# Start addresses of the matrix products' operands in SBUF: probabilities 192 bytes past a multiple of 256, token tiles 16 bytes past one

## The chip, the core and the metric

The kernel runs on one core of one Trainium2 chip. The metric is device time in microseconds of one execution; lower is better. Engines go by their short names: PE is TensorE's matrix products, PEld its loads of the stationary operand, DVE VectorE, ACT ScalarE, POOL GpSimd, SP SyncE, which issues the transfers.

## What is computed

Eight sequences of 576 tokens and eight heads of 64 columns go through an attention over 32 memories a head, and its output through a feed-forward block, all in float32:

```
a    = softmax(phi)                      # 576 x 32 a head
k_m, v_m = a^T k, a^T v                  # 32 x 64 a head
attn = softmax(q k_m^T / 8)              # 576 x 32 a head: "the probabilities"
x    = attn v_m                          # heads side by side: 4608 x 512
h    = x @ w_in                          # 512 -> 2048
out  = (h * clip(h + 3, 0, 6) / 6) @ w_out   # 2048 -> 512
```

## The kernel before, in words

For each of the 8 sequences (b) the kernel first folds the memories into the first weight matrix: `fold` (L367) multiplies v_m with a chunk of w_in, and the result, split into a high and a low part, is the tile `both` (L385, L393). So the first product can take the probabilities themselves as its moving operand.

The work is a list of 140 slots. A slot is one block of 128 of the 2048 hidden columns (index f). In 124 slots, all in one precision, these steps run:

- `gemm1` (L427) is the first product. It has 12 matrix products on PE, each with a load of a 128 by 128 stationary part of `both`: six have the probabilities of the first 256 tokens as moving operand (tiles `phi0`, `plo0`: high part, low part, 256 columns), six those of the last 320 tokens (`phi1`, `plo1`, 320 columns). For each half the order is high by high twice, low by high twice, high by low twice.
- `relu` (L449, ACT), `gate` (L453, DVE) and `gate_rest` (L459, ACT) turn the result into the gated tile `gf`, 128 by 576. The last 64 tokens of each sequence go to `rest` and are worked on later in 16 slots of their own, which have no first product.
- `high` (L468, ACT) and `low` (L473, DVE) split 512 tokens of `gf` into `ghi` and `glo`, each four token tiles of 128.
- `gemm2` (L480) is the second product, two slots later (`LAG = 2`): 12 products of 512 columns, each with a token tile of `ghi` or `glo` as the stationary operand and a part of w_out (`w2`, in the profile named `w`) as the moving one. First the four tiles of `ghi` with the high part of w_out, then the same four with its low part, then the four of `glo` with the high part.

The last four of the 16 slots of `rest` use `gemm2_by_columns` (L507) instead, with 256 columns a product: 96 products, the last work of the kernel.

The order of all steps is written out by hand: a string `BEGIN` for the start and a table `STEADY` for what is played between the steps of each slot. The first eight slots are "plain": they use unsplit float32, where each product passes twice (tiles `pT` and `gp`). A few products (`warm`, L627, bf16) fill PE at the start.

Tiles of a pool stand one behind the other in each partition of SBUF, so that a tile's start address follows from the sizes of the tiles ahead of it. In the kernel before, `threes` (16 words, of which one is used) and `maxima` (a slice of a wider tile) stand ahead of others.

Of the kernel before, what the change touches and what calls it, by code (L numbers as in the profile page):

```python
# [10 lines left out]
F32 = mybir.dt.float32  # L11
F32R = mybir.dt.float32r
# [7 lines left out]
B, H, S, D, M = 8, 8, 576, 64, 32  # L20
DM, DF = 512, 2048
P = 128
# [4 lines left out]
NG = 2  # L27
# [6 lines left out]
KV = 2 * D + 1  # L34
EPS = 1e-9
LAG = 2
VC = 256
VW_RING = {"tag": "vw", "bufs": 6}
TMP = {"tag": "tmp", "bufs": 3}
# [57 lines left out]
def attention_ffn_kernel(ctx: ExitStack, tc: tile.TileContext, pn, pt, kv, kl, qt, w1, w2, out):  # L97
    nc = tc.nc
    cpool = ctx.enter_context(tc.tile_pool(name="cpool", bufs=1))
    wpool = ctx.enter_context(tc.tile_pool(name="wpool", bufs=1))  # L100
    xpool = ctx.enter_context(tc.tile_pool(name="xpool", bufs=1))
# [29 lines left out]
    def magnitude(*u):  # L131
        sizes[u] = sb.tile([P, UNIT], U32, name="tmp", **(O_RING if u in ((1, 0), (1, 1)) else TMP))
        for cols, high, _ in raw[u]:
            nc.scalar.activation(sizes[u][:, cols].bitcast(F32), high.bitcast(F32), AF.Abs)  # L134
# [12 lines left out]
    def sign(*u):  # L147
        for cols, high, _ in raw[u]:
            size_ = sizes[u][:, cols]
            nc.vector.scalar_tensor_tensor(size_, high, 0xC0000000, size_, ALU.bitwise_and, ALU.bitwise_or)  # L150
# [55 lines left out]
    class Attention:  # L206
# [178 lines left out]
        def folded_high(self, c, k):  # L385
            both = vw[self.b, FC // VC * c + k] = wpool.tile([P, 2, NG, VC], F32R, name="both", **VW_RING)
            nc.scalar.copy(both[:, 0], self.pv[c][:, :, VC * k : VC * (k + 1)])  # L387

        def folded(self, c, k):
            both = vw[self.b, FC // VC * c + k] = wpool.tile([P, 2, NG, VC], F32R, name="both", **VW_RING)  # L390
            nc.scalar.copy(both[:, 0].bitcast(F32), self.pv[c][:, :, VC * k : VC * (k + 1)])

        def folded_low(self, c, k):  # L393
            both = vw[self.b, FC // VC * c + k]
            src = self.pv[c][:, :, VC * k : VC * (k + 1)]
            nc.vector.tensor_tensor(both[:, 1], src, both[:, 0].bitcast(F32), ALU.subtract)  # L396
# [11 lines left out]
    class Slot:  # L408
# [44 lines left out]
        def gate(self):  # L453
            relu = self.gf
            if self.plain:
                self.gf = wpool.tile([P, 4 * P], F32, name="gp", tag="ghi", bufs=LAG + 1)[:, : self.n]
            nc.vector.scalar_tensor_tensor(self.gf, relu, 6.0, self.h, ALU.min, ALU.mult)  # L457

        def gate_rest(self):  # L459
# [6 lines left out]
            return self.gf[:, : len(self.tiles) * P]  # L466

        def high(self):  # L468
            self.ghi = wpool.tile([P, 4 * P], F32R, name="ghi", tag="ghi", bufs=LAG + 1)
            nc.scalar.copy(self.ghi[:, : len(self.tiles) * P], self.gated())  # L470

        def low(self):
            self.glo = wpool.tile([P, 4 * P], F32R, name="glo", tag="glo", bufs=LAG + 1)  # L473
            n = len(self.tiles) * P
            nc.vector.tensor_tensor(self.glo[:, :n], self.gated(), self.ghi[:, :n].bitcast(F32), ALU.subtract)  # L475

# [176 lines left out]
    def play(words):  # L653
        for word in words:
            name, *args = word.split(".")
            n = [int(x) for x in args]
            if name in WEIGHTS:
                WEIGHTS[name](*n)
            elif name in SLOT:
                SLOT[name](slots[n[0]], *n[1:])  # L660
            elif name in LOADS:
                LOADS[name](*n)
            else:
                ATTENTION[name](atts[n[0]], *n[1:])
# [25 lines left out]
    def laid_out(first, last, rows):  # L690
        said = []
        for n in range(first, last):
            s = slots[n]
            said += [f"{x}.{n}" for x in ("h" if s.rest else "gumkh" if 1 in s.hfs else "gumh")]
            for w in rows.get(n, ()):
                said += group(w)
            said.append(f"l.{n}")
            if n >= LAG:
                said += [f"a.{n - LAG}"] + slots[n - LAG].ends(n - LAG)
        return said  # L700

    def table(text, start):
        rows = {}
        for line in text.split("/"):
            words_ = line.split()
            if words_:
                rows.setdefault(start + int(words_[0]), []).extend(words_[1:])
        return rows

    with tc.manual_schedule():  # L710
        ident = cpool.tile([P, P], F32, name="ident")
        make_identity(nc, ident)
        ones = cpool.tile([P, P], F32, name="ones")
        nc.vector.memset(ones, 1.0)

        threes = xpool.tile([P, M // 2], F32, name="three")
        nc.vector.memset(threes, 3.0)
        three = threes[:, :1]

        maxima = cpool.tile([P, 3 * M], F32, name="maxima")[:, : NG * M]  # L720
        nc.vector.memset(maxima, 0.0)

        rest = wpool.tile([P, NFT, P], F32, name="rest")
        nc.vector.memset(rest[:, :NJ], 0.0)  # L724

        play(BEGIN.split())
        n = starts[5]
        for b in range(2, B + 1):
            if b > 2 and b % 2 == 0:
                play(laid_out(n, n + NFT // 4, {}))  # L730
                n += NFT // 4
            if b < B:
                rows = table(STEADY.replace("C", str(b)).replace("N", str(b + 1)).replace("M", str(b + 2)), n)
                for k in rows:
                    rows[k] = [w for w in rows[k] if int(w.split(".")[1]) < B]
                play(laid_out(n, n + NFT, rows))
                n += NFT
        for k in range(n - LAG, n):
            play([f"a.{k}"] + slots[k].ends(k))
# [49 lines left out]
```

## Time and profile before

| what | us |
|---|---|
| three runs | 714.71, 714.26, 714.60; median 714.6 |
| the profiled execution | 714.73, of which span 712.9 |
| PE busy | 703.4 of 712.9 |
| PEld busy | 561.8 |
| DVE, ACT, POOL busy | 383.0, 325.7, 105.6 |
| granted TensorE clock | 1.0 over the whole span |

The profiled execution lasts 1.8 us longer than its span and 0.1 us longer than the median of the runs. A matrix product is a pipeline: its recorded length is longer than the distance to the next one's start, and its end is modelled. So a product's price is read from the distances between starts, or from a piece of the chain of waits divided by its count, and not from the mean length of one.

### The profile page before, as it was taken

To read this page: it belongs to the slowest core of one execution; us is meant where nothing else is said; L and a number is where in the kernel's file an instruction comes from. 1 tells how busy PE (TensorE), PEld (TensorE's weight loads), DVE (VectorE), ACT (ScalarE), POOL (GpSimd) and SP (SyncE) were. 2 spreads that over 40 slices of the span, in tenths; PEclk is the share of its full clock that TensorE was granted. 3 is DMA by queue.
4 is the path that set the end of the run, shared out by engine and by line. 5 is a ranking of instruction groups with operands and counts; after the bars stand their busy time and mean duration, and the time that the engine had idled before them with its cause. 6 is when DMAs were issued, how large, how long until landed. Compare 5 with 4: busy or idle time off the path is not lost.

```text
span 712.9 us, 11655 instructions
## 1 busy us (share of the span) xinstructions
PE 703.4 (99%) x4806; PEld 561.8 (79%) x4806; DVE 383.0 (54%) x593; ACT 325.7 (46%) x626; POOL 105.6 (15%) x73
## 2 busy tenths in 40 slices
PE   9999999999999999999999999999999999999997
PEld 4456777888878787878788887888888888788887
DVE  4899986765453554545534455535544354343331
ACT  4677785643343443434434344534344344443331
POOL 1645331430100310013000120002100031000000
PEclk9999999999999999999999999999999999999999
DMA  9997682645230804153320532128041211130002
GB/s 348 420 344 284 197 284 87 245 145 188 114 141 16 348 2 163 60 208 140 129 94 16 197 152 105 59 92 316 1 163 60 74 60 60 60 118 1 1 1 74
DMA packets 25149, 99.21 MB, mean 139 GB/s; under 512 B 2696, under 2 KB 3720, under 8 KB 20488
## 3 DMA queue, kind: packets, MB, share of 16 engines
q1 hardware_dynamic: 25016, 98.40, 37.0%
q8 instruction: 38, 0.62, 0.4%
q14 instruction: 15, 0.12, 0.1%
q10 hardware_dynamic: 80, 0.07, 0.0%
HBM read 82.72 MB, written 15.73 MB: 138 GB/s over the span
## 4 chain that ended last, share of the span: by engine, by line
PE 93%; DVE 4%; ACT 1%; issue 1%; POOL 1%; ACTq 0%; POOLq 0%
PE acc L497 53%; PE ph L441 28%; PE pv L376 4%; PE acc L627 3%; PE pk L271 2%; PE acc L516 2%; PE psc L309 1%; DVE gf L457 1%; DVE tmp L142 1%; ACT gf L451 0%; DVE glo L475 0%; POOL w L171 0%; PE pq L293 0%; DVE w L171 0%; DVE tmp L150 0%
## 5 line engine op out<-in xcount | busy, mean ns | idle before, releaser
L497 PE MATMUL acc<-w,ghi 128*128 128x512 f32 x1088 | 282.0, 397 | 0.0
L497 PEld LDWEIGHTS acc<-w,ghi 128*128 128x128 f32 x1088 | 197.5, 188 | 65.4 <-ACT gf L451 15.1
L457 DVE SCALAR_TENSOR_TENSOR gf<-gf,ph 128x576 f32<-128x576 f32 x124 | 93.3, 753 | 185.7 <-ACT gf L451 185.2
L451 ACT ACTIVATE gf<-ph,three 128x576 f32<-128x576 f32 (+2 forms) x132 | 95.8, 727 | 197.9 <-PE ph L441 193.0
L441 PE MATMUL ph<-phi,both 128*128 128x256 f32 x992 | 174.1, 297 | 2.1 <-DVE gf L457 2.0
L441 PEld LDWEIGHTS ph<-phi,both 128*128 128x128 f32 x992 | 150.9, 188 | 16.2 <-DVE gf L457 4.5
L497 PE MATMUL acc<-w,glo 128*128 128x512 f32 x544 | 150.3, 389 | 0.0
L497 PEld LDWEIGHTS acc<-w,glo 128*128 128x128 f32 x544 | 102.1, 188 | 21.3
L475 DVE TENSOR_TENSOR glo<-gf,ghi 128x512 fp32r<-128x512 f32 x124 | 88.5, 715 | 39.7 <-ACT ghi L470 36.6
L441 PE MATMUL ph<-plo,both 128*128 128x256 f32 x496 | 105.7, 294 | 0.0
L441 PEld LDWEIGHTS ph<-plo,both 128*128 128x128 f32 x496 | 78.5, 188 | 0.0
L470 ACT CAST ghi<-gf 128x512 fp32r<-128x512 f32 x124 | 76.0, 616 | 4.6 <-PE acc L497 3.6
L461 ACT COPY rest<-gf 128x64 f32<-128x64 f32 x124 | 30.2, 245 | 86.5 <-DVE gf L457 86.5
L396 DVE TENSOR_TENSOR both<-pv,both 128x512 fp32r<-128x512 f32 x62 | 42.7, 689 | 49.8 <-ACT both L387 49.6
L339 POOL TENSOR_TENSOR st<-st,mx 128x512 f32<-128x512 f32 (+1 forms) x16 | 22.8, 1423 | 287.6 <-DVE mx L335 287.6
L387 ACT CAST both<-pv 128x512 fp32r<-128x512 f32 x62 | 36.1, 584 | 23.6 <-DVE both L396 18.2
L376 PE MATMUL pv<-w,kvT 64*32 64x512 f32 (+1 forms) x528 | 35.1, 588 | 1.0 <-DVE pnat L254 0.6
L364 POOL TENSOR_TENSOR plo<-pT,phi 128x512 fp32r<-128x512 f32 (+1 forms) x14 | 21.3, 1526 | 56.2 <-ACT phi L359 56.2
L351 POOL TENSOR_TENSOR st<-st,sm 128x512 f32<-128x512 f32 (+1 forms) x15 | 19.6, 1304 | 63.6 <-DVE sm L347 52.2
L160 POOL TENSOR_TENSOR w<-tmp,raw 128x512 uint32<-128x512 uint32 x14 | 21.8, 1576 | 45.3 <-DVE tmp L150 24.9
L627 PE MATMUL acc<-rest,ident 128*128 128x512 bf16 x82 | 22.1, 421 | 1.7 <-DVE rest L724 1.7
L134 ACT ACTIVATE tmp<-raw 128x512 f32<-128x512 f32 (+1 forms) x24 | 18.9, 831 | 6.2 <-DMA raw<-in_w 6.2
(77 smaller groups left out, 425.7 us busy)
## 6 DMA issues: line engine op xcount, KB each, us to landing
w<-w_kept SPq DMA_DIRECT2D x24, 1024.0 KB, 6.7
kvt<-in_kv SPq DMA_DIRECT2D x32, 516.0 KB, 8.6
raw<-in_w SPq DMA_DIRECT2D x16, 512.0 KB, 8.9
raw<-in_w SPq DMA_DIRECT2D x8, 1024.0 KB, 10.2
out_t<-o SPq DMA_DIRECT2D x16, 512.0 KB, 3.0
qh<-in_qt SPq DMA_DIRECT2D x8, 640.0 KB, 10.1
ptile<-in_pt SPq DMA_DIRECT2D x8, 576.0 KB, 3.8
pnat<-in_pn SPq DMA_DIRECT2D x8, 576.0 KB, 4.7
```

Of the source, the lines that this page charges most:

```text
L339: (engine or nc.gpsimd).tensor_tensor(st, st, self.over_memories(hf, "mx"), ALU.subtract)
L376: nc.tensor.matmul(to[j * M : (j + 1) * M, g, k], self.kvT[rows, g, j * M : (j + 1) * M], chunk[rows, k, j].bitcast(F32), start=True, stop ...
L387: nc.scalar.copy(both[:, 0], self.pv[c][:, :, VC * k : VC * (k + 1)])
L396: nc.vector.tensor_tensor(both[:, 1], src, both[:, 0].bitcast(F32), ALU.subtract)
L441: nc.tensor.matmul(dst, w[:, g, fs], x[:, g * n : (g + 1) * n], start=(i == 0), stop=(i == len(seq) - 1),)
L451: nc.scalar.activation(self.gf, self.h, AF.Relu, bias=three)
L457: nc.vector.scalar_tensor_tensor(self.gf, relu, 6.0, self.h, ALU.min, ALU.mult)
L461: nc.scalar.copy(kept, self.gf[:, self.n - REST :])
L470: nc.scalar.copy(self.ghi[:, : len(self.tiles) * P], self.gated())
L475: nc.vector.tensor_tensor(self.glo[:, :n], self.gated(), self.ghi[:, :n].bitcast(F32), ALU.subtract)
L497: nc.tensor.matmul(accs[self.b, self.rest, k], left[:, t * P : (t + 1) * P], w, start=k in self.first and k not in begun, stop=k in self.l ...
L627: nc.tensor.matmul(fill["out"], ident.bitcast(BF16)[:, :P], fill["in"], start=True, stop=True)
```

## The change

No instruction is added, removed or moved on any engine; one fill at the start, of `three`, is 1 column wide where it was 16. The start addresses of tiles change, through the widths of the tiles ahead of them, and `ghi` and `glo` begin 4 words inside their tiles.

```diff
+AHEAD = 4
...
             if self.plain:
-                self.gf = wpool.tile([P, 4 * P], F32, name="gp", tag="ghi", bufs=LAG + 1)[:, : self.n]
+                self.gf = wpool.tile([P, 4 * P + 64], F32, name="gp", tag="ghi", bufs=LAG + 1)[:, : self.n]
...
         def high(self):
-            self.ghi = wpool.tile([P, 4 * P], F32R, name="ghi", tag="ghi", bufs=LAG + 1)
+            self.ghi = wpool.tile([P, 4 * P + 64], F32R, name="ghi", tag="ghi", bufs=LAG + 1)[:, AHEAD : AHEAD + 4 * P]
...
         def low(self):
-            self.glo = wpool.tile([P, 4 * P], F32R, name="glo", tag="glo", bufs=LAG + 1)
+            self.glo = wpool.tile([P, 4 * P + 64], F32R, name="glo", tag="glo", bufs=LAG + 1)[:, AHEAD : AHEAD + 4 * P]
...
-        ones = cpool.tile([P, P], F32, name="ones")
+        ones = cpool.tile([P, P + M], F32, name="ones")[:, :P]
...
-        threes = xpool.tile([P, M // 2], F32, name="three")
-        nc.vector.memset(threes, 3.0)
-        three = threes[:, :1]
-
-        maxima = cpool.tile([P, 3 * M], F32, name="maxima")[:, : NG * M]
+        three = xpool.tile([P, 1], F32, name="three")
+        nc.vector.memset(three, 3.0)
+
+        maxima = xpool.tile([P, NG * M + 40], F32, name="maxima")[:, : NG * M]
```

In the two built programs the operands of the products stand at these bytes past a multiple of 256, in each of their buffers and at each start of a part of them (the parts of a tile lie multiples of 256 bytes apart):

| operand | moving or stationary | before | now |
|---|---|---|---|
| `phi0`, `plo0` (first product, 256 columns) | moving | 64 | 192 |
| `phi1`, `plo1` (first product, 320 columns) | moving | 0 | 0 |
| `both` (first product) | stationary | 0 | 0 |
| w_out's parts (second product) | moving | 0 | 0 |
| `ghi`, `glo` (second product) | stationary | 0 | 16 |
| w_in's chunks (fold) | moving | 0 | 0 |
| `kvT` (fold, scores) | stationary | 0, 128 | 128, 0 |
| `qh` (scores) | moving | 224 | 96 |

The tiles of the attention, which stand behind all others, move up by 1664 bytes together, so `gf`, `st` and `pT`, the key and value tiles and the output tiles are 128 bytes further round.

## Rows read from the trace of the kernel before

**Rows 1.** The page's busy time, share of the span and instructions of each engine, then the granted clock in 40 slices.

```profile
PE   703.4 (99%) x4806; PEld 561.8 (79%) x4806; DVE 383.0 (54%) x593; ACT 325.7 (46%) x626; POOL 105.6 (15%) x73
...
PEclk9999999999999999999999999999999999999999
```

**Rows 2.** The page's chain that ended last, as shares of the span by line (its first entries).

```profile
PE acc L497 53%; PE ph L441 28%; PE pv L376 4%; PE acc L627 3%; PE pk L271 2%; PE acc L516 2%; PE psc L309 1%; DVE gf L457 1%; DVE tmp L142 1%; ACT gf L451 0%; DVE glo L475 0%; POOL w L171 0%; PE pq L293 0%; DVE w L171 0%; DVE tmp L150 0%
```

**Rows 3.** Groups of instructions by line and shape: operation, count, busy us, mean ns of one, idle time before.

```profile
L497 PE MATMUL acc<-w,ghi 128*128 128x512 f32 x1088 | 282.0, 397 | 0.0
L497 PE MATMUL acc<-w,glo 128*128 128x512 f32 x544 | 150.3, 389 | 0.0
L441 PE MATMUL ph<-phi,both 128*128 128x256 f32 x496 | 80.3, 284 | 2.1 <-DVE gf L457 2.0
L441 PE MATMUL ph<-plo,both 128*128 128x256 f32 x248 | 49.2, 279 | 0.0
L441 PE MATMUL ph<-phi,both 128*128 128x320 f32 x496 | 93.8, 310 | 0.0
L441 PE MATMUL ph<-plo,both 128*128 128x320 f32 x248 | 56.5, 309 | 0.0
L457 DVE SCALAR_TENSOR_TENSOR gf<-gf,ph 128x576 f32<-128x576 f32 x124 | 93.3, 753 | 185.7 <-ACT gf L451 185.2
L475 DVE TENSOR_TENSOR glo<-gf,ghi 128x512 fp32r<-128x512 f32 x124 | 88.5, 715 | 39.7 <-ACT ghi L470 36.6 <-PE acc L497 2.4
L470 ACT CAST ghi<-gf 128x512 fp32r<-128x512 f32 x124 | 76.0, 616 | 4.6 <-PE acc L497 3.6 <-DVE gf L457 0.7
L376 PE MATMUL pv<-w,kvT 64*32 64x512 f32 x496 | 33.8, 601 | 0.6 <-DVE pnat L254 0.6
L627 PE MATMUL acc<-rest,ident 128*128 128x512 bf16 x82 | 22.1, 421 | 1.7 <-DVE rest L724 1.7
```

**Rows 4.** Busy time of each engine in stretches of the span (us from its start: length, then busy us and count of PE, PEld, DVE, ACT, POOL, granted clock, DMA share, GB/s).

```profile
50.00:75.00 25.00, 24.14 (x226) 17.05 (x226) 24.22 (x37) 17.98 (x34) 9.74 (x6) 1.00 0.72 260
75.00:100.00 25.00, 23.25 (x143) 18.04 (x142) 22.69 (x33) 19.13 (x36) 9.53 (x6) 1.00 0.71 253
100.00:125.00 25.00, 24.72 (x216) 19.96 (x215) 17.66 (x26) 16.17 (x27) 5.33 (x3) 1.00 0.45 147
125.00:150.00 25.00, 25.00 (x172) 20.09 (x171) 18.92 (x23) 14.08 (x30) 12.71 (x6) 1.00 0.75 265
...
200.00:300.00 100.00, 100.00 (x755) 82.34 (x754) 50.09 (x81) 41.91 (x85) 8.50 (x6) 1.00 0.34 128
```

**Rows 5.** The timeline of PE over two whole slots in a row with nothing between them: start us, length us, line, operation, count merged into the row. The distance from one row's start to the next row's start, divided by the count, is the price of one product.

```profile
244.96 0.64 PE L441 MATMUL ph<-phi,both 128*128 128x256 f32 x4
245.43 0.40 PE L441 MATMUL ph<-plo,both 128*128 128x256 f32 x2
245.67 0.76 PE L441 MATMUL ph<-phi,both 128*128 128x320 f32 x4
246.26 0.46 PE L441 MATMUL ph<-plo,both 128*128 128x320 f32 x2
246.55 2.00 PE L497 MATMUL acc<-w,ghi 128*128 128x512 f32 x8
248.40 1.07 PE L497 MATMUL acc<-w,glo 128*128 128x512 f32 x4
249.30 0.64 PE L441 MATMUL ph<-phi,both 128*128 128x256 f32 x4
249.78 0.40 PE L441 MATMUL ph<-plo,both 128*128 128x256 f32 x2
250.01 0.76 PE L441 MATMUL ph<-phi,both 128*128 128x320 f32 x4
250.61 0.46 PE L441 MATMUL ph<-plo,both 128*128 128x320 f32 x2
250.90 2.00 PE L497 MATMUL acc<-w,ghi 128*128 128x512 f32 x8
252.74 1.07 PE L497 MATMUL acc<-w,glo 128*128 128x512 f32 x4
253.65 0.64 PE L441 MATMUL ph<-phi,both 128*128 128x256 f32 x4
```

**Rows 6.** Pieces of the chain of waits, in order of time: start us, length us, line, products in the piece. These are stretches of the second product alone: the slots of `rest`, and at the end the 96 products of 256 columns.

```profile
185.94 10.91 PE acc L497 x48
...
358.34 13.63 PE acc L497 x60
...
697.80 11.52 PE acc L516 x96
```

**Rows 7.** The timeline of PE at 23 us, columns as in rows 5: 24 warm products in bf16, 512 columns, that wait for nothing.

```profile
23.15 5.35 PE L627 MATMUL acc<-rest,ident 128*128 128x512 bf16 x24
```

## Prediction

> **What bounds the kernel now.** First the busy times: PE is busy 703.4 of 712.9 us at a granted clock of 1.0 throughout, which is the level of 2.4 GHz [rows 1]. Then the chain that ended last: 53% of it is the second product (L497) and 28% the first (L441), and no other line has over 4% [rows 2]. Then the stretches: from 125 us on PE is busy for the whole of each, while DVE and ACT are busy about half the time; only up to 125 us is PE short of work, by 0.3 to 1.8 us in each 25 [rows 4]. So nothing but the pace of PE's products counts from 125 us on, and the change can work by that pace alone: it adds and removes no instruction.
>
> The pace stands in the timeline of two slots [rows 5]. A slot takes 4.34 us (244.96 to 249.30, and 4.35 to 253.65). From starts to starts: the six products of 256 columns 0.71 us, 118.3 ns each; the six of 320 columns 0.88 us, 146.7 each; the twelve of 512 columns 2.75 us, 229 each. Of these twelve the eight with `ghi` take 1.85 us, 231 each, and the four with `glo` 0.90 us, 225 to 227 each.
>
> Is that already the least possible? The warm products in bf16 show what 512 columns cost when the stream isn't disturbed: 24 of them last 5.35 us, and one alone is recorded at 421 ns [rows 3, 7], so (5.35 - 0.42) / 23 = 214 ns. In proportion, 320 columns would take 134 and 256 columns 107. What the float32 products take above that is the quantity that this change is about, and it shows a pattern:
>
> - moving and stationary operand both at a multiple of 256: 512 columns in a long stretch of the second product take 10.91 / 48 = 227.3 and 13.63 / 60 = 227.2 ns; 320 columns 146.7; 256 columns in the tail (L516) 11.52 / 96 = 120.0 [rows 5, 6]. That is 13 ns above the undisturbed pace, in all three, whatever the number of columns. A cost per product that does not grow with its columns belongs to what happens once per product, and that is the load of its 128 stationary columns, which reads SBUF while the product before it streams.
> - moving operand at 64, stationary at 0: 256 columns take 118.3, so 11 ns above.
> - the eight products after the change from the first to the second product take 231, 4 more than in a long stretch.
>
> I read this as the stream being held up by the load that runs beside it, with a price that depends on how their addresses stand to each other. That is an inference: addresses are in no row, and only two pairings of them (0 with 0, 64 with 0) occur in this precision.
>
> **The change part by part.** Two pairings are new: the second product's goes from (0, 0) to (0, 16), the first half's of the first product from (64, 0) to (192, 0).
>
> The second product, 1088 + 544 = 1632 products [rows 3]. Upper bound of the gain: the whole excess goes, 229 - 214 = 15 ns by 1632 = 24.5 us. The other end: nothing excludes that 16 is a worse pairing than 0; the nearest dearer price is the one behind a change of product, 231 on all of them, (231 - 229) by 1632 = 3.3 us lost, and if the excess doubled, 13 ns by 1632 = 21 us lost, for which no row speaks. What I take: in the only comparison of two pairings at one width, leaving 0 was worth 120.0 - 118.3 = 1.7 ns, and I give that to every product, 2.8 us. I also let the dearer start of each slot go, because a stream that doesn't run into the load has nothing to settle into: 8 products by 4 ns by 124 slots = 4.0 us. Together 6.8 us less.
>
> The first half of the first product, 496 + 248 = 744 products [rows 3]. 192 is 64 short of a multiple where 64 is 64 past one. Between the ends of (118.3 - 107) by 744 = 8.4 us gained and, back to the price of pairing (0, 0), 1.7 by 744 = 1.3 us lost, I take 0, since the distance from the multiple is the same.
>
> The second half of the first product, 744 products, keeps its pairing: 0. The 96 products of the tail go with the second product: at 1.7 ns 0.2 us gained, at most 13 by 96 = 1.2 us.
>
> The fold (L376) keeps its moving operand, and its stationary tile goes round by 128 bytes. Its 496 products of 512 columns are unsplit float32 and run several at a time (33.8 us busy for 496 with a mean of 601 ns [rows 3]); 4% of the chain is theirs [rows 2]. I take 0; a twentieth of that share, 1.4 us either way, is the bound. Writes and reads of the moved tiles by DVE and ACT are covered: `gf`, `ghi` and `glo` cost them 753, 616 and 715 ns of a slot of 4340 [rows 3, 5], so even some tens of ns more each would stay under PE. The narrower fill of `three` is one instruction at the start: 0. If PE gets faster by 55 ns a slot (6.8 us over 124), ACT and DVE go from about half busy to half busy and one percent, and nothing is late next. Before 125 us a part of the gain is lost, since PE waits there for DVE anyway: the 75 us from 50 to 125 hold at most 75 / 4.34 = 17 of the 124 slots, 0.9 us of the gain, and I count half of that as lost.
>
> Sum: -6.8 - 0.2 + 0.5 = -6.5 us against the profiled execution's 714.7, so 708.2. The median of the runs stands 0.1 below that execution: **708** us.
>
> **The rivals.**
>
> *The load is cleared out of the stream's way altogether.* If one line of 16 bytes between the two is the step that matters, most of the excess goes: between half and all of 24.5 us in the second product, with up to 8.4 in the first half, -13 to -33 us, 682 to 702. For it: the excess is the same 13 ns at 512, 320 and 256 columns, so it looks like one cause that can be avoided. Against it: 64 bytes, a far larger step, took away 2 of the 13.
>
> *Addresses do nothing.* The 1.7 ns between tail and first half may come from the lines themselves: the tail's products write other banks and follow another order. Then the time stays within a microsecond of 714.6.
> The Trainium skill (SBUF, "Who interferes with whom") says that PE has two read ports, one for the moving operand and one for the load of the stationary one, independent of each other, and that PE never waits on anyone; by that rule this rival is the one to expect. The trace doesn't agree as it stands: a load costs the stream 13 ns here, though it does not say through which part of the memory.
>
> *Slower: 16 bytes is a start from which the stream meets the load more often.* The place is the second product, from its first slot in this precision to the end. If both advance through the same memory, the load starting one step ahead may put it just where the stream arrives; then the dear first products of a slot last for all twelve (231 or more), and the first half falls back to 120. At 231 that is 3.3 + 1.3 us, 719; at half as much excess again, 6.5 by 1632 = 10.6 us and 1.3 more, 726.5. It decides from about 1 ns more per product (1.6 us). For it: the dear start shows that this price can rise without any change of address. Against it: the one step away from 0 that the trace has made things cheaper.
>
> **How the numbers follow.** A measurement of this kernel tells changes from about 0.2%, 1.4 us. Forecast, a gain of 1.5 to 13 us (702 to 713): 0.44. All or most of the excess gone (682 to 702): 0.22. No effect, 713 to 716: 0.13. Slower, 716 to 727: 0.21. So faster 0.66, the same 0.13, slower 0.21. For a range that leaves out 2 in 10, I cut the lower half of the case of the full gain and the upper third of the slower one: 690 to 721.
>
> **What would show it.** In the profile after, the twelve products of a slot should take 2.65 to 2.70 us from start to start instead of 2.75, the pieces of 48 and 60 products 225 to 226 ns each instead of 227.3, and the eight with `ghi` should no longer be dearer than the four with `glo`; the six products of 256 columns should stay at 0.71 us, those of 320 columns at 0.88. If the long pieces fall to 215 to 220 each, the first rival is right; if a slot keeps 4.34 us, the second; if the piece of 48 is above 11.0 us, the third. The prediction is wrong as a whole if the time moves while these distances don't, for instance by a transfer or a wait before 125 us.

## The result and the profile after

| | median | range | runs |
|---|---|---|---|
| before | 714.65 us | 714.26 to 715.18 | 6 |
| after | 718.74 us | 718.20 to 719.42 | 6 |

The change makes the kernel slower: ratio 1.0058, interval 1.0045 to 1.0071, 4.1 us. The forecast was 708 us and faster. The time is that of the slower rival, 719.

Lines of the kernel after stand one further down: L442 is the first product, L498 the second, L517 the 96 products at the end. The page of the kernel after, busy times, granted clock, and the chain by engine and by line:

```profile
PE 706.8 (99%) x4802; PEld 561.0 (78%) x4806; DVE 382.7 (53%) x593; ACT 325.9 (45%) x626; POOL 105.7 (15%) x73
...
PEclk9999999999999999999999999999999999999999
...
PE 91%; DVE 4%; DMA 2%; ACT 1%; issue 1%; SPq 1%; POOL 1%; ACTq 0%; POOLq 0%
PE acc L498 53%; PE ph L442 27%; PE pv L377 4%; PE pk L272 2%; PE acc L517 2%; DMA kvt<-in_kv 1%; PE psc L310 1%; PE acc L628 1%; DVE tmp L143 1%; DMA raw<-in_w 1%; DVE gf L458 0%; DVE glo L476 0%; POOL w L172 0%; PE pq L294 0%; ACT gf L452 0%
```

The bound is the same as in [rows 1, 2]: PE, at the same clock, with 3.4 us more of busy time. DVE and ACT have not moved. The row of the stretches that answers to [rows 4] (length, then busy us and count of PE, PEld, DVE, ACT, POOL, granted clock, DMA share, GB/s) has PE without a gap again:

```profile
125.00:150.00 25.00, 25.00 (x172) 19.88 (x171) 18.38 (x23) 13.87 (x28) 12.74 (x6) 1.00 0.76 271
```

Two groups of the page (line, operation, shape and count; busy us, mean ns) answer to [rows 3]:

```profile
L498 PE MATMUL acc<-w,ghi 128*128 128x512 f32 x1088 | 285.7, 400 | 0.0
L498 PE MATMUL acc<-w,glo 128*128 128x512 f32 x544 | 153.0, 394 | 0.0
```

So it is the second product that has grown, by 3.7 and 2.7 us. How it pays shows in one slot of PE's timeline (start us, length us, what, count), as in [rows 5]:

```profile
249.98 0.64 PE L442 MATMUL ph<-phi,both 128*128 128x256 f32 x4
250.45 0.40 PE L442 MATMUL ph<-plo,both 128*128 128x256 f32 x2
250.68 0.74 PE L442 MATMUL ph<-phi,both 128*128 128x320 f32 x4
251.27 0.46 PE L442 MATMUL ph<-plo,both 128*128 128x320 f32 x2
251.56 2.03 PE L498 MATMUL acc<-w,ghi 128*128 128x512 f32 x8
253.43 1.09 PE L498 MATMUL acc<-w,glo 128*128 128x512 f32 x4
254.35 0.63 PE L442 MATMUL ph<-phi,both 128*128 128x256 f32 x4
```

From start to start the slot takes 4.37 us, 0.03 more. The first product's two halves take 0.70 and 0.88 (before 0.71 and 0.88; as medians over the kernel 707 and 876 ns, before 710 and 888), the second product 2.79 (before 2.75). The eight with `ghi` take 1.87, 234 ns each, the four with `glo` 0.92, 230 each: what were dear products at the start of a slot are now twelve dear products. The long stretches in the chain of waits (start us, length us, what, count) say it most plainly:

```profile
186.11 11.19 PE acc L498 x48
...
359.70 13.99 PE acc L498 x60
529.28 13.99 PE acc L498 x60
...
701.73 11.38 PE acc L517 x96
```

11.19 / 48 = 233.1 and 13.99 / 60 = 233.2 ns, where [rows 6] has 227.3 and 227.2. The starts of these pieces show where the loss comes in: 0.17 us by the first (185.94 before), 1.36 by the second (358.34), 3.93 by the last (697.80). From 186 us on it is spread evenly over all that PE paces. Of these stretches only that of the 96 products of 256 columns got cheaper, 118.5 ns each for 120.0.

In the tables below, times of the second product are distances between starts in the trace, as medians, sorted by what PE did just ahead of it: "plain" where that was the first product (62 times; four more, with another step right behind them, are left out), "behind another step" where it was a fold, scores or another step of the attention (49 times).

| kernel | `phi0`; tiles at | plain | behind another step |
|---|---|---|---|
| before | 64; 0 | 2749 ns | 2851 ns |
| after | 192; 16 | 2791 | 2906 |

Summed from 186 us on, each against its counterpart in the kernel before, that is 2.1 us for 50 plain ones, 2.1 for 43 others and 1.2 for the long stretches; the first product gives 1.6 back and the last 96 products 0.1. Together 3.7, and the chain shows 3.6 (3.93 - 0.17 - 0.14).

### The profile page after: what moved, and what is told of

The parts are those of the page before. It is cut to its first block, busy times and chain, and to the rows that moved or that the text cites. A ratio compares the mean times of both kernels' runs of the same rounds, so it can differ in the third digit from the quotient of the medians.

```text
span 716.7 us, 11651 instructions
## 1 busy us (share of the span) xinstructions
PE 706.8 (99%) x4802; PEld 561.0 (78%) x4806; DVE 382.7 (53%) x593; ACT 325.9 (45%) x626; POOL 105.7 (15%) x73
## 4 chain that ended last, share of the span: by engine, by line
PE 91%; DVE 4%; DMA 2%; ACT 1%; issue 1%; SPq 1%; POOL 1%; ACTq 0%; POOLq 0%
PE acc L498 53%; PE ph L442 27%; PE pv L377 4%; PE pk L272 2%; PE acc L517 2%; DMA kvt<-in_kv 1%; PE psc L310 1%; PE acc L628 1%; DVE tmp L143 1%; DMA raw<-in_w 1%; DVE gf L458 0%; DVE glo L476 0%; POOL w L172 0%; PE pq L294 0%; ACT gf L452 0%
## 5 line engine op out<-in xcount | busy, mean ns | idle before, releaser
L498 PE MATMUL acc<-w,ghi 128*128 128x512 f32 x1088 | 285.7, 400 | 0.0
L498 PEld LDWEIGHTS acc<-w,ghi 128*128 128x128 f32 x1088 | 198.4, 189 | 67.2 <-ACT gf L452 15.1
L442 PE MATMUL ph<-phi,both 128*128 128x256 f32 x992 | 172.4, 296 | 1.9 <-DVE gf L458 1.8
L442 PEld LDWEIGHTS ph<-phi,both 128*128 128x128 f32 x992 | 149.0, 188 | 16.7 <-DVE gf L458 4.4
L498 PE MATMUL acc<-w,glo 128*128 128x512 f32 x544 | 153.0, 394 | 0.0
L498 PEld LDWEIGHTS acc<-w,glo 128*128 128x128 f32 x544 | 102.8, 189 | 23.7
L442 PE MATMUL ph<-plo,both 128*128 128x256 f32 x496 | 105.9, 295 | 0.0
L442 PEld LDWEIGHTS ph<-plo,both 128*128 128x128 f32 x496 | 79.3, 188 | 0.0
L377 PE MATMUL pv<-w,kvT 64*32 64x512 f32 (+1 forms) x528 | 35.1, 588 | 0.9 <-DVE pnat L255 0.6
```

The lines of the kernel that those rows point to most:

```text
L377: nc.tensor.matmul(to[j * M : (j + 1) * M, g, k], self.kvT[rows, g, j * M : (j + 1) * M], chunk[rows, k, j].bitcast(F32), start=True, stop ...
L442: nc.tensor.matmul(dst, w[:, g, fs], x[:, g * n : (g + 1) * n], start=(i == 0), stop=(i == len(seq) - 1),)
L498: nc.tensor.matmul(accs[self.b, self.rest, k], left[:, t * P : (t + 1) * P], w, start=k in self.first and k not in begun, stop=k in self.l ...
```

## The experiments

**1. One part alone, and other starts for the token tiles.** Four kernels, all edits of one number in the changed kernel.

Only the probabilities move (tiles back at 0):

```diff
-AHEAD = 4
+AHEAD = 0
```

> The changed kernel with the token tiles back at a multiple of 256; the probabilities of the first 256 tokens stay 192 past one. Theory (two separate prices: the second product's 512-column products cost 6 ns more with the stationary at 16, the first product 15 ns less a slot with its moving operand at 192): a product in the long stretches falls back to 227 ns, 48 of them to 10.9 us, the first product keeps 1.58 us, and the time is about 2 us below the kernel before, 712.5 to 713.2. Rival (the loss comes with the shift of all the other tiles, by 128 bytes for the attention's and by 256 modulo 512 for the weights'): the long stretches stay at 233 ns and the time stays near 718.7.

Measured: 712.87 us, ratio 0.9975 (0.9966 to 0.9984). Faster by 1.8 us, as expected. The second product takes 2745 ns plain and 2853 behind another step, close to before; the first product 1582 for 1598. The long pieces of 60 are back at 13.62 us with all the other tiles still shifted, so the rival, the shift of the other tiles, is out.

Only the tiles move (probabilities back at 64):

```diff
-        maxima = xpool.tile([P, NG * M + 40], F32, name="maxima")[:, : NG * M]
+        maxima = xpool.tile([P, NG * M + 8], F32, name="maxima")[:, : NG * M]
```

> The changed kernel with the probabilities of the first 256 tokens back at 64 past a multiple of 256 (and so the attention's tiles back where they stood modulo 256); the token tiles stay 16 past. Theory (two separate prices): the second product stays at 233 ns in the long stretches, the first product goes back to 1.60 us a slot, and the time is some 2 us above the changed kernel, 720 to 721. Rival (the shift of the other tiles is the loss): near the kernel before, 714.6.

Measured: 716.32 us, ratio 1.0021 (1.0012 to 1.0030). Slower than before, but by 1.6 us only, where 720 to 721 was expected: a miss. -1.8 and +1.6 alone make +4.1 together, so prices don't add, and one price per pairing of addresses can't be the whole of it. The chain of waits of this run (start us, length us, what, count) shows why:

```profile
242.89 3.00 PE acc L498 x12
245.89 1.56 PE ph L442 x12
247.44 2.72 PE acc L498 x12
250.16 1.60 PE ph L442 x12
251.76 2.79 PE acc L498 x12
254.55 1.56 PE ph L442 x12
256.11 2.72 PE acc L498 x12
```

The same twelve products from the same kind of addresses take 2.72 us in one slot and 2.79 in the next; 33 of the 62 plain ones are at 2.72. Neither time is that of the kernel before, 2.75.

The tiles at 64 and at 32 instead of 16 (`AHEAD = 16`, `AHEAD = 8`):

> The changed kernel with the token tiles 64 bytes past a multiple of 256 in place of 16. Theory A (any start away from the moving operand's breaks a steady state that holds at equal starts, so each is dearer): 230 ns or more a product in the long stretches, 716 to 722. Theory B (the price depends on the distance, with cheap and dear ones; 64 was 2 ns cheaper than 0 for 256 columns): 222 to 226 ns, 706 to 712.

> The changed kernel with the token tiles 32 bytes past a multiple of 256 in place of 16. Theory A (any start away from the moving operand's is dearer): 230 ns or more a product in the long stretches, 716 to 722. Theory B (the price depends on the distance): something other than both 227 and 233 ns; if it rises steadily from 16 to 32, above 236 ns and above 722; if it falls towards 64, below 230 and below 717.

Measured: 718.58 us, 1.0054 (1.0040 to 1.0068), and 718.09 us, 1.0047 (1.0034 to 1.0061). Plain second products take 2803 and 2798 ns. Both times are those of theory A, and 16 isn't special as a step; but that any start away from 0 is dearer is already contradicted by half the slots of the run above.

**2. The pairings by themselves.** A kernel of products alone, with no other engine at work: 20 products from one pair of start addresses, then the next pair, for 512, 256 and 320 columns. It and the two kernels like it below ran once each.

```diff
+        for m in (0, 4):
+            for k in range(16):
+                for n in range(REPEAT):
+                    t = n % 4
+                    nc.tensor.matmul(acc[:, t], sta[k][:, t * P : (t + 1) * P], mov[m], start=n < 4, stop=n >= REPEAT - 4)
+                leave()
```

> The disputed price by itself: a kernel that leaves out the reference's work and only runs sequences of 20 float32 products, each sequence with a short wait ahead of it, the stationary operand at 0, 16, ... 240 bytes past a multiple of 256, the moving one at 0 or 64 (512 columns), at 0, 64, 128 or 192 (256 columns), at 0 (320 columns). Theory B (the settled price of a product depends on the pairing of addresses alone): at 512 columns 227 ns for (0, 0), 233 for stationary 16 and 32, 233 for 64, and the same table for any moving start when the stationary is counted from it; then one stationary start is the cheapest for all widths, and it is worth 6 to 12 ns a product below 227 if there is a cheap one. Theory C (a pairing has several steady states, and the way into the sequence chooses): prices jump between a few values (113, 117 or 120 at 256 columns; 227 or 233 at 512) without order in the stationary's start, and differ from those in the kernel at the same pairing.

PE's timeline of this run (the names tell how many bytes past a multiple of 256 the moving and the stationary operand start):

```profile
21.10 4.80 PE L50 MATMUL acc<-mov_zero,sta_sixteen 128*128 128x512 f32 x20 [0.25 <-ACT sink L44]
26.22 4.93 PE L50 MATMUL acc<-mov_zero,sta_thirtytwo 128*128 128x512 f32 x20 [0.31 <-ACT sink L44]
...
182.96 2.65 PE L56 MATMUL acc<-mov_zero,sta_zero 128*128 128x256 f32 x20 [0.31 <-ACT sink L44]
...
194.72 2.55 PE L56 MATMUL acc<-mov_zero,sta_sixtyfour 128*128 128x256 f32 x20 [0.31 <-ACT sink L44]
```

With everything else silent the addresses alone change the pace: (4.93 - 4.80) / 19 = 7 ns a product at 512 columns. The settled distances are 226.7 (moving at 0 with stationary at 16 or 240, both at 64) to 234 ns at 512 columns, 113.4 (stationary 64 bytes past moving, at three of the four moving starts) to 120.0 (equal starts, and some others) at 256, 144.5 to 146.7 at 320. Two things follow. None of the 32 pairings at 512 columns goes below 226.7. And 0 with 16, the pairing of the change, is among the cheapest here, although it is dear in the kernel. So the pairing alone doesn't set the price.

**3. Whole slots by themselves.** The twelve products of a slot's first product and the twelve of its second, six slots for each setting (`both`, `phi0`, tiles, in words of 4 bytes), no other engine at work.

```diff
+        for b, p, t in ((0, 16, 0), (0, 16, 0), (0, 48, 0), (0, 16, 4), (0, 48, 4), (16, 0, 0), (0, 0, 0)):
+            for k in range(SLOTS):
+                first_product(b, p)
+                second_product(t, k == 0, k == SLOTS - 1)
```

> PE alone: six slots in a row of first product (six of 256 columns, six of 320) and second product (twelve of 512), with nothing else running and no wait inside, for seven settings: probabilities at 64 with tiles at 0 (twice, the first while the clock may still rise), 192 with 0, 64 with 16, 192 with 16, then the folded weights at 64 with probabilities and tiles at 0, and last all at 0. It leaves out the reference's work. Theory (the pace is settled by PE's own stream and its loads, and a pairing can have two steady states between which the products ahead of it choose): once settled a slot takes 4.35 us for 64 and 0, 4.33 for 192 and 0, 4.37 for 192 and 16, and for 64 and 16 either about 4.29 or 4.38, as in the whole kernels; with the folded weights at 64 about 4.31; with all at 0 4.35. Rival (other engines' reads and writes of SBUF hold the stream up): without them every setting takes about the same, near 4.1 us.

Measured: the settled slots take 4347 ns with 64 and 0 (before), 4327 with 192 and 0, 4373 with 192 and 16 (after), the same as in the whole kernels, whose slots take 4347, 4327 and 4373. Other engines and transfers have no part in it, and that rival is out. The six products of 320 columns, none of whose own addresses differ, take 887 ns behind probabilities at 64 and 875 behind probabilities at 192. With the folded weights at 64 the slot takes 4333 ns, where 4310 was expected. With 64 and 16 there is no single settled slot (PE's timeline of this run):

```profile
95.27 0.87 PE L47 MATMUL h<-phi_sixtyfour,both_zero 128*128 128x256 f32 x6
95.97 1.05 PE L49 MATMUL h<-last_zero,both_zero 128*128 128x320 f32 x6
96.86 2.95 PE L53 MATMUL acc<-w_zero,tiles_sixteen 128*128 128x512 f32 x12
99.65 0.84 PE L47 MATMUL h<-phi_sixtyfour,both_zero 128*128 128x256 f32 x6
100.33 1.04 PE L49 MATMUL h<-last_zero,both_zero 128*128 128x320 f32 x6
101.21 2.88 PE L53 MATMUL acc<-w_zero,tiles_sixteen 128*128 128x512 f32 x12
103.93 0.87 PE L47 MATMUL h<-phi_sixtyfour,both_zero 128*128 128x256 f32 x6
```

2.79 us (96.86 to 99.65), then 2.72 (101.21 to 103.93), and so on in turn. The addresses are the same in both; what differs is how the products ahead went (the six of 256 columns 0.70 and 0.68 us, those of 320 columns 0.89 and 0.88). So the sequence carries something over from product to product, which I call its state.

**4. Other addresses for the first product.** The folded tile `both` at 64, with the probabilities and tiles at 0; and everything at 0.

```diff
+    def folded_tile():
+        n = 2 * NG * VC
+        both = wpool.tile([P, n + 64], F32R, name="both", **VW_RING)
+        return both[:, BOTH_AT : BOTH_AT + n].rearrange("p (k g v) -> p k g v", k=2, g=NG)
```

> Folded weights (the first product's stationary operand) 64 bytes past a multiple of 256, all other operands of the two products at a multiple: the pairing that settled at 113.4 ns for 256 columns by itself, beside 117.8 for the one of the kernel before. Theory (prices measured alone hold in the kernel): 256 columns settle at 113 to 115 ns, a slot is 20 to 30 ns shorter than in the kernel before, and the time is 711 to 712.5, the fastest so far. Rival (how the sequence is entered decides): the six products of 256 columns stay at 117 to 120 and the time is within 1.5 us of 714.6.

> All operands of the two products at a multiple of 256, the probabilities of the first 256 tokens too. Theory (prices by pairing): 256 columns at 120 ns in place of 118.3, no dearer start of the 320 columns behind them, since the pairing doesn't change there; 1.3 us lost on the first and 0.9 to 1.2 gained on the second: 714 to 716. Rival (leaving the multiple was worth more, because a change of pairing resets the sequence): above 717.

Measured: 713.55 us, 0.9983 (0.9974 to 0.9992), a miss by 1 us; and 714.52 us, 0.9998 (0.9989 to 1.0007), as expected, though by smaller terms: the products of 256 columns are 3 ns a slot dearer (713 for 710), those of 320 columns 6 cheaper (882 for 888), the second product 4 cheaper. The miss has the same cause as that of experiment 1: I carried the 113.4 ns of 20 products in a row over to six products behind the second one, and there they take 117 to 118.

**5. All settings of a slot.** The same whole slots, five each, for 209 settings of `phi0`, `phi1` and the tiles (in words).

```diff
+SETTINGS = [(16, 0, 0)] + [(p, 0, t) for t in (0, 4, 8, 12, 16, 32, 48, 52, 56, 60) for p in range(0, 64, 4)]
+SETTINGS += [(p, q, t) for q in (16, 32, 48) for t in (0, 4, 16, 60) for p in (0, 16, 32, 48)]
```

> PE alone, five slots in a row without a wait for each of 209 settings (start of the probabilities of the first 256 tokens and of the last 320, and of the token tiles, in steps of 16 bytes or more past a multiple of 256; folded weights and w_out's parts at a multiple). It leaves out the reference's work. Theory (a slot settles into an orbit that depends on all the pairings together): the settled slot takes between 4.25 and 4.45 us, the settings that were run as whole kernels come out as they did (4347 ns for 64 and 0, 4327 for 192 and 0, 4373 for 192 and 16, 4278 and 4389 in turn for 64 and 16), and a few settings settle below 4.30 for good. Rival (prices add up pairing by pairing): the slot's time is the sum of one part that depends on the probabilities' start alone and one that depends on the tiles' start alone, to 5 ns.

Measured: the five settings above come out with the same slots again. With the tiles at 16 the settled slot ranges from 4293 to 4387 ns depending on where `phi0` starts; the tiles at 0 give only 4320 to 4353. So neither operand has a price of its own, and the rival, prices that add up, is out. A few settings below 4300 were expected; one settles there for good (4293, `phi0` at 144). Close behind is 4300 ns with 32 and 16, in bytes. PE's timeline of that setting:

```profile
446.92 0.86 PE L44 MATMUL h<-phi,both 128*128 128x256 f32 x6
447.62 1.04 PE L47 MATMUL h<-last,both 128*128 128x320 f32 x6
448.50 2.88 PE L52 MATMUL acc<-w,tiles 128*128 128x512 f32 x12
451.22 0.86 PE L44 MATMUL h<-phi,both 128*128 128x256 f32 x6
```

The second product takes 2.72 us here in every slot, with the tiles where the change puts them.

**6. The cheap setting in the whole kernel.** `phi0` at 32, or at 224, with the tiles at 16 as in the change.

```diff
-        maxima = xpool.tile([P, NG * M + 40], F32, name="maxima")[:, : NG * M]
+        maxima = xpool.tile([P, NG * M], F32, name="maxima")[:, : NG * M]
```

> The change with the first half's probabilities at 32 instead of 192 (the pad behind the maxima goes); token tiles at 16 as in the change. Theory (the price belongs to the settled sequence of a whole slot; PE alone settled at 4300 ns for this setting, against 4347 for the kernel before): a plain slot takes 4.30 us, the second product 2.73 us in it; up to 47 ns by 124 slots = 5.8 us are gained, less 0.9 us in the 144 products of long stretches, which stay at 233 instead of 226.7: 709.5 to 712 us, at most 0.996 of before. Rival (in the whole kernel scores, folds and gaps come between slots, and from each the sequence falls back into the dear one): plain slots at 4.37 us or a mixture, 714 to 718 us, 0.999 or more.

> The same with the first half's probabilities at 224 (a pad of 48 words). PE alone settled at 4307 ns. Theory: a plain slot takes 4.31 us, 40 ns by 124 = 5.0 us gained less 0.9: 710.5 to 713 us. Rival (the sequence falls back into the dear one): 714 to 718 us. Were it the token tiles' 16 alone that costs, as the changed kernel beside the kernel before would suggest at first sight, both of these would be at 717 or more.

Measured: 713.98 us, 0.9991 (0.9982 to 1.0000), and 714.11 us, 0.9990 (0.9981 to 0.9999). Both numbers of the theory missed, and by time alone the rival is the nearer one. The chain of waits of the first (start us, length us, what, count) shows that both are half right:

```profile
241.14 1.02 PE pv L377 x16
242.16 3.00 PE acc L498 x12
245.16 1.59 PE ph L442 x12
246.74 2.72 PE acc L498 x12
249.46 1.58 PE ph L442 x12
251.04 2.72 PE acc L498 x12
```

The plain slots do take 4.30 us, and 61 of the 62 second products in them 2.72. But the second product behind a fold (L377) takes 3.00 (2.94 at the same place in the kernel before): twelve dear products, from the same addresses, in the same kernel, one slot before twelve cheap ones. By starts the 49 behind another step have a median of 2906 ns, 55 more than before: 62 by 29 ns gained, 49 by 55 lost, and the first product's 18 ns a slot turn that small loss into the small gain.

**7. Addresses chosen by what comes ahead.** Taken one by one, the distances of the twelve plain products in the kernel before are 231, 231, 236, 228, 233 and 231 ns, then 227 to the end, as medians; in the changed kernel they stay at 232 to 236 up to the eleventh; with 32 and 16 all twelve take 227, but behind a fold 338 and then 232 to 235. So at 16 the second product would have two settled states, and what comes ahead decides which; at 0 it would have one, which takes some six dear products to reach. Which step ahead leads into which state I had found by trying, not derived. Then the tiles should be at 16 only where the first product comes straight ahead (`BEHIND_OTHER` lists the other slots; `phi0` stays at 32).

```diff
+            self.at = 0 if len(highs) in BEHIND_OTHER else AHEAD
+            highs.append(self)
+            self.ghi = wpool.tile([P, 4 * P + 64], F32R, name="ghi", tag="ghi", bufs=LAG + 1)
+            self.ghi = self.ghi[:, self.at : self.at + 4 * P]
```

> Probabilities of the first half at 32 as in the run before; token tiles at 16 in the 71 slots whose second product comes straight behind the first one, at 0 in the 50 whose second product comes behind another step (fold, scores, memories) and in the 15 behind a second product. Theory (at 16 the second product has two settled states, 226.7 and about 233 ns a product, and what came just ahead of it decides which; at 0 it has one, 226.7, reached after some six dear products whatever came ahead): the 62 plain slots keep 2.72 us for their second product, as with 16 throughout, and the 49 behind another step fall from 2.91 to 2.85 us, as with 0 throughout: 2.5 us less than the run before, 711.0 to 712.3 us, 0.9955 of before. Rival (the state is carried on from slot to slot, so that a plain slot behind a slot at 0 starts in the dear one): second products of 2.79 us in the plain slots too, 714 to 716 us.

Measured: 711.34 us, ratio 0.9950 (0.9936 to 0.9964), 3.6 us faster than before and 7.4 than the change. It held. The chain of waits of this run (L384 is the fold, L511 the second product):

```profile
240.93 1.02 PE pv L384 x16
241.95 2.94 PE acc L511 x12
244.90 1.58 PE ph L451 x12
246.48 2.72 PE acc L511 x12
249.20 1.58 PE ph L451 x12
250.78 2.72 PE acc L511 x12
```

Eight of the kernels side by side, with the first product (66 of them between two second products) and the long pieces of 60:

| kernel | `phi0`; tiles at | plain, ns | behind another step, ns | first product, ns | 60 products, us | us |
|---|---|---|---|---|---|---|
| before | 64; 0 | 2749 | 2851 | 1598 | 13.63 | 714.65 |
| all at 0 | 0; 0 | 2745 | 2854 | 1595 | 13.63 | 714.52 |
| only probabilities | 192; 0 | 2745 | 2853 | 1582 | 13.62 | 712.87 |
| after | 192; 16 | 2791 | 2906 | 1582 | 13.99 | 718.74 |
| only tiles | 64; 16 | 2720 or 2790 | 2906 | 1560 to 1600 | 13.99 | 716.32 |
| tiles at 32 | 192; 32 | 2798 | 2900 | 1575 | 14.00 | 718.09 |
| 32 and 16 | 32; 16 | 2720 | 2906 | 1580 | 13.60 | 713.98 |
| by what is ahead | 32; 16 or 0 | 2720 | 2853 | 1580 | 13.60 | 711.34 |

## Why the prediction was wrong

**What bounds the kernel**: right. PE is busy for 25.00 of 25 us from 125 us on in the kernel after too, and the loss is in the distances between its starts. That a part of the change is lost up to 125 us was right as well: PE's starts are 0.34 us earlier than before at 50 us and 0.20 earlier at 125 us, so these 75 us cost 0.14 us, where the next 61 us cost 0.37.

**That the addresses set the excess**: half right. Moving one operand alone moves the pace with every other engine silent (experiment 2), so the second rival, no effect, is out. A page of the Trainium skill, SBUF — State Buffer ("Who interferes with whom"), has PE's two read ports independent and PE waiting on no one; by it these 7 ns a product would not be expected, and the trace does not agree with it in this precision, though no run shows through which part of the chip they come. But the excess over bf16 can't be taken away by an address either: none of the pairings went below 226.7 ns at 512 columns, 11 above the warm products. (From start to start those stand 216 ns apart; the prediction's 214 came from a row's length, whose end is modelled.) That rules the first rival out too. Nor is the excess the same at every width, as the prediction read it: beside 216 ns, and in proportion 135 at 320 columns and 108 at 256, the cheapest settled distances are 226.7, 144.5 and 113.4, so 10.7, 9.5 and 5.4 more. The prediction's even 13 ns set the cheapest settled distance at 512 columns beside dear ones at the other widths (146.7 and 120.0); that the excess is a fixed cost of the load was argued from it, not shown.

**The step that failed** is the second product's term. It had two parts. "Leaving 0 was worth 120.0 - 118.3 = 1.7 ns, and I give that to every product": the one comparison behind it, [rows 5] against [rows 6], was of products of 256 columns, and there it held (118.5 for 120.0 in the last 96, 0.14 us gained, 0.2 forecast). At 512 columns there was no cheaper place to go, only a dearer one: 233. "I also let the dearer start of each slot go, because a stream that doesn't run into the load has nothing to settle into": the opposite happened. The dear products at the start of a slot in the kernel before, six by their distances, were a way into the one settled state that it has with tiles at 0; with 16 there are two, and behind the first product with `phi0` at 192, as behind every fold, PE stays in the dear one. Instead of 6.8 us gained, 5.4 were lost from 186 us on. The hoped-for gain exists, but it hangs on what comes ahead: with `phi0` at 32 (experiment 6) the dear start of a plain slot does go, 29 ns where the forecast had 8 by 4.

**The first product**, both halves taken as 0: mis-sized, and mostly in the half whose own addresses stay. The first half gains 3 ns a slot (710 to 707), 0.4 us. The second half, which "keeps its pairing: 0", gains 12 (888 to 876), 1.5 us: behind a half at 64 its first two products are dearer (157 and 149 ns) than behind one at 192 (149 and 140). Together they are the gain of 1.8 us for the probabilities alone. Neither "the distance from the multiple is the same" nor the unchanged pairing was a reason: what runs ahead enters into the price.

**The fold and the other engines at 0**: right. A fold takes 1.02 us in the chain before and after; `gf`, `ghi` and `glo` cost DVE and ACT 753, 616 and 713 ns (before 753, 616, 715).

**The slower rival** named the mechanism, "the dear first products of a slot last for all twelve", and its price of 231 gave 719. Its details were off both ways: the dear state costs 233, and the first product did not lose 1.3 us but gained 1.6. That the sum met the measured time is luck: the two errors cancel. I gave it 0.21 because the only step away from 0 in the trace had made things cheaper; that step was at another width, and the dear start in [rows 5] was the better witness.

## What to carry to other kernels

A price per instruction that is read where a stream has settled holds for that stream only: try a changed operand in the whole repeating sequence, with what comes ahead of it, before multiplying by a count. Products alone reproduced the plain slots of three kernels to the nanosecond, but their sequences held no slot behind a fold or another interruption; the sequence to measure has to hold those too. And a run of dear instructions behind a change of work can be a sign, as it was here, that there is more than one state, so that a change can make it longer as well as shorter.

## What was not expected of the hardware

- In this float32 precision, the pace of products that each load their own stationary operand depends on the start addresses of both operands within 256 bytes, varied in steps of 16: 226.7 to 234 ns at 512 columns, 113.4 to 120.0 at 256, with only PE at work and the clock granted at 1.0.
- From the same addresses the stream has more than one settled pace (2.72 and 2.79 us for twelve products), and what ran just ahead decides which; it can hold for 60 products (13.60 or 13.99 us) or alternate from slot to slot.
- Open: through which part of the chip the two operands meet, whether the load of the stationary operand is what waits, and whether the accumulators' banks or the higher bits of the addresses have a share. No run varied those by themselves.
